# Second layer norm, denominators and Strassen-like factors of an adaLN block: some work moved between VectorE and GpSimd, some begun at other steps

## The chip, the core and the metric

The kernel runs on one core of one Trainium2 chip, in one launch. The metric is the device time of that launch in microseconds (us); smaller is better. Five engines work side by side, each with its own queue in order: TensorE (PE in the profile; its weight loads are PEld), VectorE (DVE), ScalarE (ACT), GpSimd (POOL) and SyncE (SP), which here only issues DMA transfers. An instruction at the head of a queue that waits holds up all that stands behind it on that queue.

## The reference

For a token matrix `x` of 2048 x 512 and a condition vector `c`, all in float32:

```
sa, ca, ga, sb, cb, gb = six rows of 512, from silu(c) @ w_mod
h = layernorm(x) * (1 + ca) + sa
q, k, v = h @ wqkv, in 32 heads of 16
pq, pk = phi(q), phi(k)          # phi(t) = (t + 1 if t > 0 else exp(t)) + 1e-6
kv, z = pk^T v, sum of pk        # per head, over all tokens
o = (pq kv) / (pq z + 1e-6)
x = x + ga * (o @ wo)
h = layernorm(x) * (1 + cb) + sb
x = x + gb * (((h @ w_gate) * (h @ w_up)) @ w_down)     # 1376 hidden columns
```

The attention is linear: keys and values are summed up over all tokens first, and only then are the queries used.

## The kernel before

**Precision.** Every float32 product is made of three matmuls on operands split in a high part (a rounded copy, made on ScalarE, line 181) and a low part (source minus high part, line 182, on VectorE or, where `low=` or `on=` says so, on GpSimd). A "split" below is this pair of instructions; a "low" is its second half.

**Tokens.** The 2048 tokens are 16 token tiles of 128, in 4 chunks of 4 tiles. Token tile i is tile i mod 4 of chunk i / 4.

**First stage.** First layer norm, keys and the sums over tokens. The change leaves it as it is.

**Query stage.** For each token tile: the query product (`proj`, 12 matmuls), `q_a` and `q_b` (phi, on ScalarE and VectorE), then the denominator. `den_q` (lines 511 and 485) multiplies phi with the summed keys, on GpSimd; `den_t` (lines 503 to 509) is three VectorE instructions: the sum by head (L491), the constant added (L508), the reciprocal (L509); `den_c` (L520) divides phi by the denominator, on VectorE. For chunk 0 the denominators are made earlier in another way.

**The y steps.** `y_step(i)`, line 633, is written out by hand for i = 0 to 11. In the order of the program it has: if asked for, the query product of a later tile; the turning of tile i+1 (`turn_a`, 4 transposes, L591, which need `den_c(i+1)`); `pre` and `pe` extras; `den_c(i+2)`; the output product of tile i (`y_a`, 12 matmuls, L616); high and low part of the turned tile i+1 (L595 on ScalarE, L599 on VectorE); `mid` extras; `y_b(i-1)`, which takes tile i-1 out of PSUM and makes the statistics of the second layer norm (L225, L226 on VectorE); the preload of the next accumulator (L604); and `after` extras. The lists of extras are where most of the change is made. The order of calls is the order on each queue; no scheduler changes it.

**Second layer norm.** `rstd_of` (lines 228 to 234) adds epsilon on VectorE (L233) and takes the power -0.5 on GpSimd (L234). `nmr_of` (L237) makes minus mean times rstd, on VectorE. `xhat` (L243) applies both on ScalarE. `ln2_turn` transposes 4 normalized tiles (L250), `ln2_f` (L670) scales and shifts them; chunks 2 and 3 are stored to HBM (`kept`) and read back.

**Gated products.** The two gated products are done together by a Strassen-like scheme with seven products in place of eight, in 22 blocks (`block`, line 794): two sides of 2 chunks each (side 0 is chunks 0 and 1), times 11 hidden tiles f, in groups of 2, 2, 2, 2 and 3. A side has seven left factors for two indices k: `a11`, `s1`, `s2`, `a12`, `s3`, `a22`, `s4`, where s1 to s4 are sums of quarters (`Left.sum`, L698) and each is split (`Left.split`, L181 and L182). A block has seven right factors, made of weights: `right_load`, `right_sums` (4 instructions on GpSimd, L748), `right_split` (4 high parts on ScalarE, L759 and L762; 4 lows on GpSimd, L766). In a block PE runs, 6 matmuls each (L780), the products with a11, s1, s2, a12, s3, then `pe` extras (down products of an earlier group among them, L858 to L860), then a22 and s4. Four PSUM banks hold the partial results and are copied from one to the next (L786); L832, L841 and L806 on VectorE combine them. The points `a11`, `s1`, `s2`, `s3`, `pe`, `mid`, `s4` of a block take extras from the dictionary `early` and from the loop at line 1011: `at[point]` is a list of things to issue there.

**Down products.** The rows of `w_down` are scaled at `s4` of a block (L875, VectorE) and split at `s2` of the next (`split_down`, line 966): high part on ScalarE, low part on GpSimd. `down` takes its sums out of PSUM on VectorE (L865).

**The second side.** While side 0 is being worked on, the left factors of side 1 are made in small steps (`trickle`; `some(n)` issues the next n steps) and stored in HBM (`stash`); around the change of sides (blocks 10 and 11) `fetch` reads them back. All tiles of 128x512 come from one pool of 99; a new tile waits for the last user of the one whose place it takes.

## Time and profile before

| | us |
|---|---|
| median of 3 runs (579.56 to 579.96) | 579.6 |
| the profiled execution, whole | 582.47 |
| its span, first to last instruction | 580.8 |
| PE busy in the span | 563.6 |
| VectorE busy | 376.3 |
| ScalarE busy | 294.2 |
| GpSimd busy | 236.1 |

The profile is of one execution. Its whole time is 1.67 us over its span, and 2.87 us over the median of the runs. An engine's busy time is an average over stages with different limits, so the views that matter are those by stretch of time (busy time of each engine, and the granted TensorE clock, from the span's start), the waits of PE by what ended them, the chain of work that ended last, and the order of time on single engines. Rows of groups and of the order of time give the line, engine and operation, then `out<-in` by the tiles' names, the shape and a count.

### The profile page before, as it was taken

How to read it: one execution, taken by the hardware profiler on the slowest of the kernel's cores; microseconds unless marked ns; L12 is line 12 of the kernel's file. 1: busy time of each engine (PE TensorE's matmuls, PEld its weight loads, DVE VectorE, ACT ScalarE, POOL GpSimd, SP SyncE). 2: the span in 40 equal slices, each digit the busy share in tenths (PEclk: the TensorE clock that was granted, in tenths of full speed). 3: DMA queues.
4: the chain of work that ended last, by engine and by line, in shares of the span. 5: the costliest groups of instructions: out<-in, count | busy, mean ns of one | idle time of the engine just before them, and what ended most of it. 6: DMA issues, size and time to landing. Idle time of an engine off the chain costs nothing.

```text
span 580.8 us, 7362 instructions
## 1 busy us (share of the span) xinstructions
PE 563.6 (97%) x2549; PEld 457.6 (79%) x2549; DVE 376.3 (65%) x622; ACT 294.2 (51%) x530; POOL 236.1 (41%) x237
## 2 busy tenths in 40 slices
PE   8999999999998998899999998999999999999997
PEld 6778888888777886688888886877888888888775
DVE  6886868868998688973544797564434444444643
ACT  3785766455556586553545447454323444333530
POOL 2000000005234225566564656397346666665320
PEclk9999999999998998999999999999999999999999
DMA  8900124202330011123024416599515121200003
GB/s 281 368 3 6 68 77 141 74 1 72 96 87 1 1 38 35 37 72 111 36 73 143 147 59 223 210 330 378 169 58 174 36 74 36 78 0 1 1 1 144
DMA packets 49109, 57.24 MB, mean 99 GB/s; under 512 B 6384, under 2 KB 26864, under 8 KB 49072
## 3 DMA queue, kind: packets, MB, share of 16 engines
q1 hardware_dynamic: 49072, 56.77, 30.1%
q8 instruction: 20, 0.33, 0.2%
q14 instruction: 17, 0.14, 0.1%
HBM read 43.12 MB, written 13.63 MB: 98 GB/s over the span
## 4 chain that ended last, share of the span: by engine, by line
PE 78%; DVE 12%; DMA 5%; ACT 2%; POOL 1%; issue 1%; SPq 1%; DVEq 0%; POOLq 0%
PE bank L780 31%; PE acc L859 7%; PE acc L860 7%; PE acc L858 7%; PE bank L196 5%; PE bank L194 5%; PE bank L195 5%; DVE h L182 3%; PE acc L616 2%; PE acc L327 2%; PE acc L325 2%; PE acc L326 2%; DMA h<-side_s 2%; DMA raw<-in_A_wqkv_dram 2%; PE bank L250 1%; DVE h L520 1%
## 5 line engine op out<-in xcount | busy, mean ns | idle before, releaser
L780 PE MATMUL bank<-h,w 128*128 128x512 f32 (+1 forms) x924 | 219.2, 392 | 4.5 <-DVE h L182 2.5
L780 PEld LDWEIGHTS bank<-h,w 128*128 128x128 f32 (+1 forms) x924 | 170.2, 186 | 46.8 <-DVE h L182 4.6
L786 ACT ACTIVATE bank<-bank 128x512 f32<-128x512 f32 (+1 forms) x44 | 25.6, 581 | 143.6 <-PE bank L780 143.5
L182 POOL TENSOR_TENSOR w<-raw,w 128x512 fp32r<-128x512 f32 (+1 forms) x22 | 36.8, 1675 | 116.0 <-ACT w L181 116.0
L806 DVE TENSOR_TENSOR phi<-bank,g 128x512 f32<-128x512 f32 (+1 forms) x22 | 15.2, 689 | 91.3 <-PE bank L780 91.3
L859 PE MATMUL acc<-w,kh 128*128 128x512 f32 (+1 forms) x176 | 69.3, 394 | 2.5 <-POOL w L182 2.5
L858 PE MATMUL acc<-w,kh 128*128 128x512 f32 (+1 forms) x176 | 69.3, 394 | 0.0
L860 PE MATMUL acc<-w,kl 128*128 128x512 f32 (+1 forms) x176 | 69.2, 393 | 0.0
L766 POOL TENSOR_TENSOR w<-raw,w 128x256 fp32r<-128x256 f32 (+3 forms) x44 | 45.0, 1023 | 38.2 <-ACT w L759 38.1
L766 POOL TENSOR_TENSOR w<-t,w 128x512 fp32r<-128x512 f32 (+1 forms) x44 | 57.9, 1317 | 0.0
L865 DVE TENSOR_TENSOR x<-acc,x 128x512 f32<-128x512 f32 x80 | 50.3, 681 | 9.2 <-PE acc L860 9.2
L234 POOL TENSOR_TENSOR rstd<-ve,half 128x4 f32<-128x4 f32 (+3 forms) x12 | 10.6, 883 | 106.6 <-DVE ve L233 102.4
L194 PE MATMUL bank<-w,h 128*128 128x512 f32 x120 | 48.1, 401 | 0.0
L196 PE MATMUL bank<-w,h 128*128 128x512 f32 x120 | 47.1, 392 | 0.0
L195 PE MATMUL bank<-w,h 128*128 128x512 f32 x120 | 46.7, 389 | 0.0
L485 POOL TENSOR_TENSOR f<-h,zb 128x512 f32<-128x512 f32 x12 | 17.2, 1450 | 63.7 <-ACT zb L465 50.9
L616 PE MATMUL acc<-w,xh 128*128 128x512 f32 x128 | 42.3, 412 | 0.0
L832 DVE TENSOR_TENSOR g<-bank,u 128x512 f32<-128x512 f32 (+1 forms) x22 | 15.1, 689 | 40.8 <-ACT u L786 38.9
L859 PEld LDWEIGHTS acc<-w,kh 128*128 128x128 f32 (+1 forms) x176 | 33.5, 190 | 10.0 <-POOL w L182 2.9
L858 PEld LDWEIGHTS acc<-w,kh 128*128 128x128 f32 (+1 forms) x176 | 33.5, 190 | 7.3
L860 PEld LDWEIGHTS acc<-w,kl 128*128 128x128 f32 (+1 forms) x176 | 33.3, 189 | 7.1
L243 ACT ACTIVATE n<-x,nmr,rstd 128x512 f32<-128x512 f32 x32 | 24.7, 807 | 25.9 <-DVE nmr L237 25.9
(149 smaller groups left out, 1038.7 us busy)
## 6 DMA issues: line engine op xcount, KB each, us to landing
x<-in_A_x_dram SPq DMA_DIRECT2D x24, 256.0 KB, 5.4
raw<-in_w_mod_dram SPq DMA_DIRECT2D x24, 256.0 KB, 3.6
raw<-in_B_w_gate_dram SPq DMA_DIRECT2D x40, 128.0 KB, 2.6
raw<-in_B_w_up_dram SPq DMA_DIRECT2D x40, 128.0 KB, 2.8
raw<-in_B_w_down_dram SPq DMA_DIRECT2D x20, 256.0 KB, 3.2
side_s<-h SPq DMA_DIRECT2D x16, 256.0 KB, 3.1
h<-side_s SPq DMA_DIRECT2D x16, 256.0 KB, 5.5
out_dram<-x SPq DMA_DIRECT2D x16, 256.0 KB, 2.6
```

What stands on the lines that cost most here:

```text
L182: (low or nc.vector).tensor_tensor(l, src, f32(h), op=ALU.subtract)
L194: nc.tensor.matmul(ps, ah, bh, start=i == 0, stop=False)
L195: nc.tensor.matmul(ps, ah, bl, start=False, stop=False)
L196: nc.tensor.matmul(ps, al, bh, start=False, stop=i == n - 1)
L616: nc.tensor.matmul(yps[i], x, y, start=fresh and k + n == 0, stop=k == KD - 1 and n == 2, skip_group_check=True)
L766: sub = lambda out, x, y: (on or nc.gpsimd).tensor_tensor(out, x, f32(y), op=ALU.subtract)
L780: mm = lambda x, y, **kw: nc.tensor.matmul(ps, x[:, k], y, skip_group_check=True, **kw)
L786: nc.scalar.activation(out, x, AF.Copy)
L858: nc.tensor.matmul(dn[j], hh[:n, a:b], dh[:n], start=i == 0, stop=False)
L859: nc.tensor.matmul(dn[j], hh[:n, a:b], dl[:n], start=False, stop=False)
L860: nc.tensor.matmul(dn[j], hl[:n, a:b], dh[:n], start=False, stop=i == n_of - 1)
L865: nc.vector.tensor_tensor(xt, dn[j], xt, op=ALU.add)
```

## The change

- `rstd_of` has a new argument `aside`. With it, VectorE also makes minus the mean (`nm`), and GpSimd makes `nmr` as `nm` times `rstd`, right behind the power. All calls of the second layer norm use it, and its calls of `nmr_of` and `ln2_m` go away.
- `den_c(1)` is issued before the second pair of `wo` products, where `den_c(0)` already stands. `den_t` is called for at most one token tile a step: tiles 5 and 7 come one step later than before, tile 8 two steps, tiles 9 to 12 one; the `den_q` calls are set to match.
- The sums and the split of the right factor of block 1 are issued in y steps 5 and 6; before, in y step 10 and in block 0.
- The left factors of side 0: `a11` is split in y steps 7 and 8 (before: 9); all sums s3 and s4 are on GpSimd (before: those of k = 0); s3 is summed in steps 9 and 10 and split ahead of block 0 (before: in block 0 at `s1` and `s2`); a22 is split at `s1` and `s2` (before: `s3`), s4 at `pe`, ahead of `y_a(13)`.
- The low part of the down weights is made on VectorE.
- The left factors of side 1: `a11` and `a12` are loaded in block 3 and split in blocks 3 and 4; `a21` and `a22` are loaded at `s2` of block 5; the other steps run two at a time at `s3` (from block 5 on) and at `s4` (from block 5 on). Before, everything was loaded at `s4` of block 5, and three steps ran at `s4` and, from block 6 on, at `s1`.
- The read-back around the change of sides: `a11` and `a12` in block 9, `s1`, `s2`, `s3`, `a22`, `s4` at `a11`, `s1` and `s2` of block 10.

```diff
-        def rstd_of(self, a=0, b=NJ):
+        def rstd_of(self, a=0, b=NJ, aside=False):
...
+            if aside:
+                nc.vector.tensor_scalar(self.nm[:, a:b], self.mv[:, a:b, 0], -1.0, None, op0=ALU.mult)
             nc.gpsimd.tensor_tensor(self.rstd[:, a:b], self.ve[:, a:b], half[:, a:b], op=ALU.pow)
+            if aside:
+                nc.gpsimd.tensor_tensor(self.nmr[:, a:b], self.nm[:, a:b], self.rstd[:, a:b], op=ALU.mult)
...
     q_a(9, ps)
-    den_c(0)
+    den_c(0, 1)
     w_out(2, 3)
...
-            todo = [lambda: [self.get(n) for n in ("a21", "a22", "a11", "a12")]]
-            todo += [lambda n=n: self.sum(n) for n in ("s1", "s3", "s2", "s4")]
-            return todo + [lambda n=n: self.split(n) for n in SIDE]
+            todo = [lambda n=n: self.sum(n) for n in ("s1", "s3", "s2", "s4")]
+            return todo + [lambda n=n: self.split(n) for n in ("s1", "s2", "s3", "a22", "s4")]
...
-    den_c(1)
     q_a(11, ps)
...
-    y_step(0, after=[lambda: q_b(11), lambda: den_q(7), lambda: den_t(4, 5), lambda: right_sums(0)])
-    y_step(1, after=[lambda: den_q(8), lambda: den_t(6, 7)])
-    y_step(2, after=[lambda: right_split(0), lambda: den_t(8)])
-    y_step(3, after=[lambda: n2[0].rstd_of(0, 3), lambda: den_q(9, 10)])
+    y_step(0, after=[lambda: q_b(11), lambda: den_q(7), lambda: den_t(4), lambda: right_sums(0)])
+    y_step(1, after=[lambda: den_t(5), lambda: den_q(8)])
+    y_step(2, after=[lambda: den_t(6), lambda: den_q(9), lambda: right_split(0)])
+    y_step(3, after=[lambda: den_t(7), lambda: n2[0].rstd_of(0, 3, True)])
     reload_x(8, 9, 10, 11)
-    y_step(4, q=12, pre=[lambda: n2[0].nmr_of(0, 3)], after=[lambda: n2[0].rstd_of(3, 4), lambda: n2[0].xhat(0, 1, 2), lambda: den_t(9), lambda: n2[0].nmr_of(3, 4), lambda: den_q(11)])
-    y_step(5, pre=[lambda: n2[0].xhat(3)], after=[lambda: den_t(10), lambda: den_q(12)])
-    y_step(6, pe=[lambda: ln2_turn(0, 0, 1)], after=[lambda: ln2_f(0, 0, 1), lambda: den_t(11)])
+    y_step(4, q=12, after=[lambda: n2[0].rstd_of(3, 4, True), lambda: n2[0].xhat(0, 1, 2), lambda: den_t(8), lambda: den_q(10, 11)])
+    y_step(5, pre=[lambda: n2[0].xhat(3)], after=[lambda: den_t(9), lambda: den_q(12), lambda: right_sums(1)])
+    y_step(6, pe=[lambda: ln2_turn(0, 0, 1)], after=[lambda: ln2_f(0, 0, 1), lambda: den_t(10), lambda: right_split(1)])
...
-    y_step(7, q=13, pe=[lambda: ln2_turn(0, 2, 3)], after=[lambda: n2[1].rstd_of(0, 3), lambda: ln2_f(0, 2, 3), lambda: den_t(12)])
...
-    y_step(8, pre=[lambda: n2[1].nmr_of(0, 3)], after=[lambda: n2[1].rstd_of(3, 4), lambda: den_q(13), lambda: n2[1].xhat(0, 1, 2), lambda: n2[1].nmr_of(3, 4)])
+    y_step(7, q=13, pe=[lambda: ln2_turn(0, 2, 3)], after=[lambda: n2[1].rstd_of(0, 3, True), lambda: ln2_f(0, 2, 3), lambda: den_t(11), lambda: L[0].split("a11")])
+    y_step(8, after=[lambda: n2[1].rstd_of(3, 4, True), lambda: den_q(13), lambda: n2[1].xhat(0, 1, 2), lambda: den_t(12), lambda: L[1].split("a11")])
     y_step(9, q=14, pre=[lambda: n2[1].xhat(3)], pe=[lambda: ln2_turn(1, 0, 2)], mid=[lambda: ln2_f(1, 0, 2)],
-           after=[lambda: [L[k].split("a11") for k in range(KH)], lambda: L[0].sum("s1"), lambda: den_t(13)])
+           after=[lambda: L[0].sum("s1"), lambda: den_t(13), lambda: L[0].split("a12"), lambda: L[0].sum("s3", on=nc.gpsimd)])
     y_step(10, pe=[lambda: ln2_turn(1, 1, 3)], mid=[lambda: ln2_f(1, 1, 3)],
-           after=[lambda: right_sums(1), lambda: den_q(14), lambda: L[1].sum("s1"), lambda: L[0].split("s1"), lambda: L[0].sum("s2")])
+           after=[lambda: den_q(14), lambda: L[1].sum("s3", on=nc.gpsimd), lambda: L[1].sum("s1"), lambda: L[0].split("s1"), lambda: L[0].sum("s2")])
     y_step(11, q=15, mid=[lambda: L[1].split("s1"), lambda: L[1].sum("s2")],
-           after=[lambda: L[0].split("s2"), lambda: L[0].split("a12"), lambda: den_t(14), lambda: n2[2].rstd_of(0, 3)])
-    L[0].sum("s3", "s4", on=nc.gpsimd)
+           after=[lambda: L[0].split("s2"), lambda: L[0].sum("s4", on=nc.gpsimd), lambda: den_t(14)])
     y_b(11)
     L[1].split("s2", "a12")
-    L[1].sum("s3", "s4")
+    L[1].sum("s4", on=nc.gpsimd)
+    n2[2].rstd_of(0, 3, True)
+    for k in range(KH):
+        L[k].split("s3")
...
-        split_d[s, f] = split_raw(raw_d.pop((s, f)), low=nc.gpsimd)
+        split_d[s, f] = split_raw(raw_d.pop((s, f)))
...
-        (0, "s1"): [lambda: L[0].split("s3"), lambda: turned(13), lambda: ln2_r(2, 3, 4)],
-        (0, "s2"): [lambda: L[1].split("s3")],
-        (0, "s3"): [lambda: [L[k].split("a22") for k in range(KH)]],
-        (0, "pe"): [lambda: y_a(13), lambda: [L[k].split("s4") for k in range(KH)], lambda: y_b(12)],
-        (0, "mid"): [lambda: den_q(15), lambda: den_c(14), lambda: ln2_m(2), lambda: ln2_x(2, 0)],
+        (0, "s1"): [lambda: turned(13), lambda: L[0].split("a22"), lambda: ln2_r(2, 3, 4)],
+        (0, "s2"): [lambda: L[1].split("a22")],
+        (0, "pe"): [lambda: [L[k].split("s4") for k in range(KH)], lambda: y_a(13), lambda: y_b(12)],
+        (0, "mid"): [lambda: den_q(15), lambda: den_c(14), lambda: ln2_x(2, 0)],
...
-        (3, "s2"): [lambda: ln2_m(3), lambda: ln2_x(3, 0)],
+        (3, "s2"): [lambda: ln2_x(3, 0)],
...
+        if s == 0 and n == 3:
+            second = [Left(sides[1], k).aside(stash) for k in range(KH)]
+            at["a11"].append(lambda: [l.get(x) for x in ("a11", "a12") for l in second])
+            trickle.extend(lambda x=x, l=l: l.split(x) for x in ("a11", "a12") for l in second)
         if s == 0 and n == 5:
-            second = [Left(sides[1], k).aside(stash) for k in range(KH)]
+            at["s2"].append(lambda: [l.get(x) for x in ("a21", "a22") for l in second])
             trickle.extend(x for pair in zip(*(l.steps() for l in second)) for x in pair)
-        if s == 0 and n > 5:
-            at["s1"].append(lambda: some(3))
-        if s == 0 and n >= 5:
-            at["s4"].append(lambda: some(3))
+        if s == 0 and n >= 3:
+            at["s3"].append(lambda: some(2))
+            at["s4"].append(lambda: some(2 if n > 4 else 0))
         if n:
             at["s3"].append(lambda n=n: right_split(n + 1))
-        else:
-            at["s2"].append(lambda: right_split(1))
...
+        if s == 0 and n == 9:
+            after_side = {}
+            at["pe"].append(lambda: fetch(stash, after_side, "a11", "a12"))
...
-            after_side = {}
-            fetch(stash, after_side, "a11", "s1")
-            at["a11"].append(lambda: fetch(stash, after_side, "s2", "a12"))
-            at["s2"].insert(0, lambda: fetch(stash, after_side, "s3"))
-            at["s3"].insert(0, lambda: fetch(stash, after_side, "a22", "s4"))
+            at["a11"].append(lambda: fetch(stash, after_side, "s1", "s2"))
+            at["s1"].insert(0, lambda: fetch(stash, after_side, "s3"))
+            at["s2"].insert(0, lambda: fetch(stash, after_side, "a22", "s4"))
```

More of the change, by code (lines that the diff above doesn't have):

```diff
@@ L232, in rstd_of @@
                 self.ve = T(small, "ve", (P, NJ))
+                self.nm = T(small, "nm", (P, NJ))
             nc.vector.tensor_scalar(self.ve[:, a:b], self.mv[:, a:b, 1], EPS_LN, None, op0=ALU.add)
+            if aside:
+                nc.vector.tensor_scalar(self.nm[:, a:b], self.mv[:, a:b, 0], -1.0, None, op0=ALU.mult)
             nc.gpsimd.tensor_tensor(self.rstd[:, a:b], self.ve[:, a:b], half[:, a:b], op=ALU.pow)
+            if aside:
+                nc.gpsimd.tensor_tensor(self.nmr[:, a:b], self.nm[:, a:b], self.rstd[:, a:b], op=ALU.mult)
         def nmr_of(self, a=0, b=NJ):
@@ L928, in tile_adaln_block @@
+    y_step(5, pre=[lambda: n2[0].xhat(3)], after=[lambda: den_t(9), lambda: den_q(12), lambda: right_sums(1)])
+    y_step(6, pe=[lambda: ln2_turn(0, 0, 1)], after=[lambda: ln2_f(0, 0, 1), lambda: den_t(10), lambda: right_split(1)])
+    for k in range(KH):
+        lefts[k] = Left((0, 1), k).into(side)
     right_load(2)
     reload_x(12, 13, 14, 15)
-    y_step(7, q=13, pe=[lambda: ln2_turn(0, 2, 3)], after=[lambda: n2[1].rstd_of(0, 3), lambda: ln2_f(0, 2, 3), lambda: den_t(12)])
-    for k in range(KH):
-        lefts[k] = Left((0, 1), k).into(side)
@@ L940, in tile_adaln_block @@
-    L[0].sum("s3", "s4", on=nc.gpsimd)
+           after=[lambda: L[0].split("s2"), lambda: L[0].sum("s4", on=nc.gpsimd), lambda: den_t(14)])
     y_b(11)
     L[1].split("s2", "a12")
-    L[1].sum("s3", "s4")
+    L[1].sum("s4", on=nc.gpsimd)
+    n2[2].rstd_of(0, 3, True)
+    for k in range(KH):
+        L[k].split("s3")
     trickle = []
@@ L977, in ln2_r @@
     def ln2_r(ch, a=0, b=NJ):
-        norm2[ch].rstd_of(a, b)
+        norm2[ch].rstd_of(a, b, True)
     def ln2_m(ch, a=0, b=NJ):
```

## The prediction, written before the changed kernel was built or run

> **What bounds the kernel now.** I read the page's busy times first, then busy time by stretch, then PE's waits.
>
> ```profile
> PE 563.6 (97%) x2549; PEld 457.6 (79%) x2549; DVE 376.3 (65%) x622; ACT 294.2 (51%) x530; POOL 236.1 (41%) x237
> ```
>
> PE is busy 563.6 of 580.8 us and the change leaves its matmuls alone. So it can win only PE's idle time (17.2 us) and time in which PE ran slowly. By stretch (after the length: busy time of PE, PEld, DVE, ACT, POOL, then the granted clock):
>
> ```profile
> 155.00:185.00 30.00, 27.06 (x134) 21.76 (x133) 26.90 (x51) 18.55 (x34) 11.87 (x10) 0.99 0.19 54
> 221.00:242.55 21.55, 17.28 (x65) 12.01 (x64) 19.44 (x27) 10.51 (x20) 15.66 (x13) 0.92 0.06 15
> 352.00:367.00 15.00, 12.51 (x48) 9.76 (x47) 8.46 (x15) 8.85 (x18) 9.50 (x8) 0.89 0.71 256
> ```
>
> PE idles 2.94 us in the y steps (A), 4.27 us around block 0 (B), 2.49 us in block 8 (C): 9.70 us. The other 7.5 us lie outside these stretches, which the change touches but not to PE's gain. Who ended the waits (total, times, longest):
>
> ```profile
> PE bank L591 <- DVE h L520: 2.9, 3, 1.9
> PE bank L780 <- DVE h L182: 2.5, 4, 1.3
> PE acc L859 <- POOL w L182: 2.5, 1, 2.5
> PE bank L780 <- DVE g L841: 1.5, 1, 1.5
> ```
>
> A waits for the division by the denominator, B for lows of left factors and for a bank that VectorE frees late, C for the low of a down weight on GpSimd. Each idle time is followed by a stretch at half clock:
>
> ```profile
> 181.11:184.52 3.41, 1.49 (x10) 1.01 (x9) 2.76 (x4) 1.18 (x2) 2.18 (x2) 1.00 0.00 0
> 184.52:187.94 3.42, 3.42 (x15) 3.03 (x14) 3.17 (x8) 3.42 (x8) 0.00 (x0) 0.50 0.02 5
> 225.48:228.90 3.42, 1.84 (x6) 0.67 (x4) 3.42 (x6) 2.77 (x7) 0.93 (x2) 1.00 0.00 0
> 228.90:232.31 3.41, 3.16 (x8) 2.49 (x9) 1.47 (x3) 3.13 (x7) 3.41 (x4) 0.50 0.00 0
> 358.61:362.02 3.41, 0.97 (x4) 0.84 (x5) 1.85 (x4) 3.26 (x7) 3.41 (x3) 1.00 0.81 284
> 362.02:365.43 3.41, 3.41 (x9) 2.64 (x9) 0.00 (x0) 0.11 (x1) 3.38 (x3) 0.50 1.06 405
> ```
>
> Where PE was busy for 1.84 us or less of 3.41, the next 3.41 us ran at clock 0.50, which costs half of them: 1.71 us each, 5.13 in all. The Trainium skill, "TensorE: Matmul & The Clock Gate", Part 1, says that the clock is halved after an idle window of about 3.4 us; by that, gaps of at most 2.49 us would not have halved it, these stretches would have another cause, and the sum below would be 5.13 us smaller. Here 1.58 us of idle time in a window were followed by it, so I go by the rows.
>
> **A: y steps.** The price of a step, from the chain of work (start, us, what):
>
> ```profile
> 161.90 0.60 DVE den L491
> 163.11 0.56 DVE den L491
> 164.27 0.54 DVE h L520
> 164.81 0.59 DVE xl L599
> 165.41 0.61 DVE st L225
> 166.23 0.58 DVE den L491
> 196.75 0.44 PE bank L591 x4
> 197.19 2.77 PE acc L616 x12
> ```
>
> A `den_t` costs 1.21 us (161.90 to 163.11), `den_c` and the turned low 0.6 each, the statistics 0.82. A step with one `den_t` keeps VectorE for 3.2 us, and PE for 0.44 + 2.77 = 3.2: level. Before, steps 0 to 2 carry five `den_t`, so VectorE is behind by two of them. Then GpSimd comes in:
>
> ```profile
> 176.27 1.25 DVE L237 SCALAR_TENSOR_TENSOR nmr<-mv,rstd 128x3 f32<-128x3 f32 x1 [0.96 <-POOL rstd L234]
> 180.80 1.31 DVE L508 TENSOR_TENSOR den<-den,den 128x32 f32<-128x32 f32 x1
> 182.42 0.88 DVE L237 SCALAR_TENSOR_TENSOR nmr<-mv,rstd 128x1 f32<-128x1 f32 x1
> 186.78 0.19 DVE L508 TENSOR_TENSOR den<-den,den 128x32 f32<-128x32 f32 x1
> 180.77 2.52 POOL L485 TENSOR_TENSOR f<-h,zb 128x512 f32<-128x512 f32 x2
> L234 POOL TENSOR_TENSOR rstd<-ve,half 128x1 f32<-128x1 f32 x3 | 2.0, 682 | 6.0 <-DVE ve L233 6.0
> ```
>
> L508 takes 0.19 us alone and 1.31 beside GpSimd's two L485 (1.26 each): a VectorE instruction with two inputs in SBUF stands until the GpSimd one is through.
>
> *`den_c(1)` ahead:* 0.6 us leave this queue and go to the `wo` products, where PE had no gap; if that cover is short, it costs at most the same 0.6. *One `den_t` a step:* one fewer up to step 3, 1.2 us. *`nmr` on GpSimd:* the two L237 above (2.13 us, nearly all waiting) leave VectorE; two `nm` of some 0.15 come. The GpSimd `nmr` is not in the trace: between 0.1 (all but free behind the power) and 0.7 us (L234); I take 0.5, nearest in shape. It stands behind the power it needs, so ScalarE's xhat gets it sooner than through VectorE's queue; cover gone (GpSimd late), xhat waits. That is 0.6 + 1.2 + 2.1 - 0.3 = 3.6 us against 2.94 of idle time.
>
> What is late next: `den_c(7)`. Without the first two gaps (1.02 us) PE wants the turn of tile 7 at 184.05 - 1.92 - 1.02 = 181.1. Before, that step's L508 started at 180.80; the phi ahead of it follows PE, so it starts some 1.1 sooner, at 179.7, and `den_c(7)` half a microsecond later at about 180.1, if nothing is in its way. But `den_q(10, 11)` are now both queued on GpSimd there: one wait of up to 1.26 and its own 0.6 give an end at 181.9. I leave a gap of 0.8 (ends: 0, and 1.9 as now). A wins 2.94 - 0.8 = 2.14.
>
> **B: left factors.** VectorE in block 0 before:
>
> ```profile
> 224.85 1.77 DVE L698 TENSOR_TENSOR s<-f,f 128x512 f32<-128x512 f32 x1
> 231.64 3.30 DVE L182 TENSOR_TENSOR h<-f,h 128x512 fp32r<-128x512 f32 x2
> 234.87 2.91 DVE L182 TENSOR_TENSOR h<-s,h 128x512 fp32r<-128x512 f32 x2
> 232.66 1.74 POOL L766 TENSOR_TENSOR w<-t,w 128x512 fp32r<-128x512 f32 x1
> ```
>
> Five instructions of 0.6 took 8.0 us, so 5 us went to standing behind GpSimd (sums of the left factor, then split and sums of right factors). After, the split and sums of block 1's right factor (four L766, four L748) are 40 us earlier, the s3 and s4 sums are off VectorE, and a11, a12, s3 are split before they are due. By count (0.6 an instruction, 0.8 the statistics, 1.2 a `den_t`) VectorE has about 4.0, 5.0, 3.8, 5.6 us in steps 8 to 11 and 3.4 after them, 21.8 us. PE has 20.1 in these steps (six products of 12 at 2.77, four turnings at 0.44, two layer-norm turnings at twice that) and another 9 (38 matmuls of 0.23, one turning) until s3 is wanted: 7 us to spare. GpSimd has four sums, two `den_q` and two small pairs there, some 9 us; all of it on VectorE's back would just use that up. Both banks for L841 are then freed in time, as in later blocks.
>
> What is late next: before the turn of chunk 1's tiles in step 9, ScalarE has one more split (about 0.6) ahead of the last xhat, and GpSimd the whole right split ahead of that chunk's power; I leave 0.5 (ends 0 and 2.5). B wins 4.27 - 0.5 = 3.77.
>
> The Trainium skill, "GPSIMD Engine Reference", § 4.1, would have two-input elementwise work on VectorE, GpSimd being about twice as slow, which speaks against the moved sums; by the rows a sum on GpSimd costs its 1.3 to 1.7 us off PE's path.
>
> **C: down lows and second side.** The chain into C's gap:
>
> ```profile
> 354.44 1.26 DVE h L182 x3
> 356.17 0.69 DVE raw L875
> 356.88 0.64 ACT w L181
> 357.59 3.41 POOL w L182
> ```
>
> Three low parts of the second side stand before the scaling, that before the ScalarE split, and GpSimd's low then takes 3.41 us (a free one 1.3) since VectorE's own lows keep it out. After: two steps there, scaling 0.6 earlier (355.57), then block 7's two lows, and the down low on VectorE at about 357.4 to 358.1. PE wanted it at 361.05 - 2.49 = 358.56. So C goes, with 0.5 in hand; if that fails by one GpSimd instruction, 0.8 returns. The 22 lows put 22 x 0.6 = 13 us on VectorE, which has a third of its time free, and leave GpSimd to the right factors. Behind each stands block work (L832) that waits for PE anyway. C wins 2.49.
>
> *Loads.* a21 and a22 are now wanted by sums at `s3` of block 5, while the load must follow a store made at `s2`:
>
> ```profile
> f<-kept SPq DMA_DIRECT2D x8, 256.0 KB, 4.5
> SPq L740 <- PE bank L780: 43.3, 5, 21.5
> ACT h L181 <- DMA side_a<-h: 6.7, 2, 3.4
> ```
>
> VectorE stands at these sums until the data is there, and behind it are L806 and L841, which PE wants before the third product of block 6: from the `s2` point that is 54 matmuls (a12, s3, 24 of the down product, a22, s4, a11) of 0.23, 12.4 us. Two ScalarE instructions (some 1.4), a store (I take no more than the load), a load of 4.5, two sums and two products of 0.6 make 12.8. I leave 0.5 (ends 0, for a shorter store, and 2.5, one wait of 1.3 behind GpSimd for each sum). On SP, the right factor loads queued behind these (and behind the early stores of blocks 3 and 4) come later, by up to a block; they are wanted another block after that. The earlier read-back (8 of 28 loads before block 10) takes load off SP where the old one is dense; PE lost 0.2 there, and I count nothing.
>
> **The sum.** 2.14 + 3.77 + 2.49 - 0.5 = 7.9 of idle time, and 5.1 of half clock, if no remaining gap fills its window: 13.0 us. The profiled execution took 582.5 (span 580.8); it would take 569.5. It lies 2.9 above the median of the runs, so the runs go from 579.6 to 566.6. Floor: 9.70 + 5.13 = 14.8, 564.8.
>
> **Rivals.** *GpSimd's queue becomes the wait* (0.24). From step 4 to 7 it has three `den_q`, four sums (below), four lows and then chunk 1's power, `nmr` behind it: 7 x 1.3 + 4 x 0.79 = 12.3 us in a row alone, 15.3 where the larger take the contended 1.74.
>
> ```profile
> L748 POOL TENSOR_TENSOR t<-raw,t 128x256 f32<-128x256 f32 x40 | 31.6, 789 | 1.6
> ```
>
> Then xhat comes 2.5 us late for step 9's turn, with a half-clock stretch of 1.7, and step 5 loses another 1: about 571.5. For it: L766 at 1.74 above. Against: rivals for the port on VectorE are only two a step there.
>
> *The half clock stays* (0.08), by the rule above or because what is left of the gaps still fills a window: 566.6 + 5.1 = 571.7. Against: all three stretches follow a gap.
>
> *VectorE stays behind* (0.06): the waits just move to the next low or division, and two thirds of the gain is lost: 575 to 579.
>
> *Slower: tiles run out* (0.08). Early splits and loads hold places of the 99 longer; engines then wait for PE to free a tile, in blocks 3 to 10. It decides from 13.0 / 8 = 1.6 us a block; at 2.5 the kernel takes 587. For it: SP and even ScalarE already wait for places (the last two rows above). Against: SP's waits there end long before the data is wanted.
>
> **Numbers.** The forecast, all three gaps mostly gone, has 0.54, with 564.5 to 569 as its own range. A measurement can tell about 0.2% (1.2 us) from no change. Faster: 0.54 + 0.24 + 0.08 + 0.05 = 0.91; within 0.2%: 0.01; slower: 0.08. The range 564.5 to 574 leaves out the last two rivals.
>
> **What would show it.** Right: no wait of PE for L520 over 1 us, none for left lows in block 0, none for w L182 in block 8; clock 1.00 in all three places; L508 mostly near 0.2. Wrong: PE waiting for n L243, for s L698 of GpSimd, or for L841 in block 5; ScalarE or VectorE waiting for places; half-clock stretches at new places.

## The result and the profile after

The changed kernel takes 565.6 us (median of four runs, 564.3 to 567.7) against 579.8 us for the kernel before beside it: a ratio of 0.9754, 95% interval 0.9718 to 0.979. It is faster by 2.5%. A second comparison gave 0.9752 (0.9722 to 0.9782). The forecast was 566.6 us, its range 564.5 to 574.0.

The profiled execution took 566.38 us, its span is 564.6. The span and the busy times of the changed kernel, from its page:

```profile
span 564.6 us, 7390 instructions
PE 556.7 (99%) x2549; PEld 456.0 (81%) x2549; DVE 380.2 (67%) x643; ACT 293.8 (52%) x530; POOL 207.0 (37%) x224
```

PE's idle time fell from 17.2 to 7.9 us. Busy times by stretch, columns as in the prediction, for the three places as they now lie (y steps, block 0, block 8) and for two stretches at the start:

```profile
155.00:185.00 30.00, 30.00 (x151) 24.41 (x150) 27.20 (x54) 20.97 (x40) 13.18 (x13) 1.00 0.19 54
215.00:236.00 21.00, 21.00 (x98) 17.39 (x97) 18.51 (x36) 14.30 (x26) 7.99 (x10) 1.00 0.10 26
338.00:353.00 15.00, 15.00 (x68) 12.43 (x67) 10.41 (x17) 8.26 (x16) 7.78 (x8) 1.00 0.51 181
13.27:16.68 3.41, 2.81 (x19) 2.28 (x20) 3.12 (x6) 0.63 (x1) 0.00 (x0) 1.00 1.05 386
16.68:20.09 3.41, 3.41 (x11) 2.73 (x11) 2.87 (x7) 2.82 (x5) 0.00 (x0) 0.50 1.05 386
```

In all three places PE is busy without a break and the clock is 1.00. Against that, a half-clock stretch stands at 16.68 that the profile of before did not have. All of PE's waits that are left, in the waits of the changed kernel:

```profile
PE acc L141 <- DVE w L136: 2.0, 1, 2.0
PE bank L262 <- ACT n L248: 0.9, 1, 0.9
PE acc L164 <- DVE f L159: 0.6, 1, 0.6
PE bank L784 <- DMA h<-side_s: 0.2, 1, 0.2
```

The first of these is the time before the first matmul, and the next two lie in the first 16 us. Nearly all the rest of the idle time is the 4.0 us after the last matmul. (Behind the new lines L591 is L596, L616 is L621, L780 is L784, L841 is L845, L520 is L525, L698 is L703, L859 is L863.)

**Where the time came from.** Both kernels have the same 2549 matmuls in the same order, so the k-th of one trace can be held against the k-th of the other. The difference goes from 0 to +2.0 by 18 us and settles at +1.4 (the stretch at the start), then falls to -3.4 over the y steps (A, 4.8 us), to -11.0 through block 0 (B, 7.6 us), from -11.2 to -15.8 in block 8 (C, 4.6 us), and ends at -16.1. That is 17 us from the three places and 1.4 given back at the start. The shown idle times and stretches of the prediction make 14.8 of it. Each wait costs about 0.16 us more than the view shows, because a matmul is drawn 0.39 us long while they start every 0.23; over the ten waits of the three places that is 1.6 us. The last half microsecond I cannot place, nor the other half by which the end, -16.1, lies beyond the three places.

How the critical steps now stand, from the order of time of the changed kernel, taken engine by engine (start, us, engine and line, and in brackets the idle time before and what ended it):

```profile
180.11 0.22 POOL L239 TENSOR_TENSOR nmr<-nm,rstd 128x1 f32<-128x1 f32 x1
180.29 4.25 POOL L490 TENSOR_TENSOR f<-h,zb 128x512 f32<-128x512 f32 x3
...
180.09 0.19 DVE L513 TENSOR_TENSOR den<-den,den 128x32 f32<-128x32 f32 x1
180.31 0.35 DVE L514 RECIPROCAL den<-den 128x32 f32<-128x32 f32 x1
180.58 1.55 DVE L525 SCALAR_TENSOR_TENSOR h<-h,den 128x512 f32<-128x512 f32 x1
...
182.28 0.63 PE L596 MATMUL bank<-ident,h 128*128 128x128 f32 x4
...
198.71 0.82 ACT L248 ACTIVATE n<-x,nmr,rstd 128x512 f32<-128x512 f32 x1 [0.24 <-POOL nmr L239]
...
305.99 2.48 DVE L703 TENSOR_TENSOR s<-f,f 128x512 f32<-128x512 f32 x2 [3.35 <-DMA f<-kept]
...
345.95 0.68 DVE L182 TENSOR_TENSOR w<-raw,w 128x512 fp32r<-128x512 f32 x1
```

nmr on GpSimd takes 0.22 us here, 0.20 for the first three tiles. The division of tile 7 (L525) still stands behind GpSimd's product L490, 1.55 us for 0.6, but ends at 182.13, and PE takes the turned tile at 182.28 without a wait. The fourth tile's xhat of chunk 1 ends at 199.53, 0.3 us ahead of its turn. In block 5 VectorE stands 3.35 us for the loads and PE still does not wait. The low of the down weight takes 0.68 us on VectorE.

### The profile page after: what moved, and what is told of

It is laid out like the page before. It is cut to its first block, busy times and chain, and to the rows that moved or that the text cites. A ratio compares the mean times of both kernels' runs of the same rounds, so it can differ in the third digit from the quotient of the medians.

```text
span 564.6 us, 7390 instructions
## 1 busy us (share of the span) xinstructions
PE 556.7 (99%) x2549; PEld 456.0 (81%) x2549; DVE 380.2 (67%) x643; ACT 293.8 (52%) x530; POOL 207.0 (37%) x224
## 4 chain that ended last, share of the span: by engine, by line
PE 92%; DMA 3%; DVE 3%; SPq 0%; issue 0%; ACT 0%; POOL 0%
PE bank L784 36%; PE acc L621 8%; PE acc L862 7%; PE acc L863 7%; PE acc L864 7%; PE bank L194 5%; PE bank L196 5%; PE bank L195 5%; PE acc L332 2%; PE acc L330 2%; PE acc L331 2%; PE bank L255 2%; DMA h<-side_a 1%; PE bank L596 1%; DMA x<-in_A_x_dram 1%; DMA h<-side_s 1%
## 5 line engine op out<-in xcount | busy, mean ns | idle before, releaser
L784 PE MATMUL bank<-h,w 128*128 128x512 f32 (+1 forms) x924 | 216.3, 391 | 0.2 <-DMA h<-side_s 0.2
L784 PEld LDWEIGHTS bank<-h,w 128*128 128x128 f32 (+1 forms) x924 | 170.6, 185 | 39.5 <-DMA h<-side_s 1.0
L770 POOL TENSOR_TENSOR w<-raw,w 128x256 fp32r<-128x256 f32 (+3 forms) x44 | 46.3, 1051 | 158.4 <-ACT w L763 151.1
L862 PE MATMUL acc<-w,kh 128*128 128x512 f32 (+1 forms) x176 | 68.6, 390 | 0.0
L863 PE MATMUL acc<-w,kh 128*128 128x512 f32 (+1 forms) x176 | 68.6, 390 | 0.0
L490 POOL TENSOR_TENSOR f<-h,zb 128x512 f32<-128x512 f32 x12 | 17.1, 1441 | 69.4 <-ACT zb L470 50.8
L621 PE MATMUL acc<-w,xh 128*128 128x512 f32 x128 | 40.7, 399 | 0.0
L863 PEld LDWEIGHTS acc<-w,kh 128*128 128x128 f32 (+1 forms) x176 | 33.1, 188 | 6.9
L752 POOL TENSOR_TENSOR t<-raw,t 128x256 f32<-128x256 f32 (+1 forms) x44 | 36.9, 838 | 1.7
```

Of the source, the lines that this page charges most:

```text
L621: nc.tensor.matmul(yps[i], x, y, start=fresh and k + n == 0, stop=k == KD - 1 and n == 2, skip_group_check=True)
L752: sub = lambda out, x, y: (on or nc.gpsimd).tensor_tensor(out, x, y, op=ALU.subtract)
L770: sub = lambda out, x, y: (on or nc.gpsimd).tensor_tensor(out, x, f32(y), op=ALU.subtract)
L784: mm = lambda x, y, **kw: nc.tensor.matmul(ps, x[:, k], y, skip_group_check=True, **kw)
L862: nc.tensor.matmul(dn[j], hh[:n, a:b], dh[:n], start=i == 0, stop=False)
L863: nc.tensor.matmul(dn[j], hh[:n, a:b], dl[:n], start=False, stop=False)
```

## The experiments

Each kernel is named by its label. Times are medians, with the ratio to the kernel before and its 95% interval where the kernel was timed in rounds; the kernel before had medians of 579.6 to 580.5 beside them. The diffs show only a part of each edit, and `...` stands for lines left out. First, the four parts of the change alone.

### y_only: the y steps alone

```diff
-    y_step(1, after=[lambda: den_q(8), lambda: den_t(6, 7)])
+    y_step(1, after=[lambda: den_t(5), lambda: den_q(8)])
...
-    y_step(3, after=[lambda: n2[0].rstd_of(0, 3), lambda: den_q(9, 10)])
+    y_step(3, after=[lambda: den_t(7), lambda: n2[0].rstd_of(0, 3, True)])
```

> The kernel before with only the edits to the y steps: nmr of the second layer norm on GpSimd, and the denominators' order per token tile. Theory (the three idle places are independent, and each brings its own half-clock stretch): the gaps in the y steps and the stretch after them go, the gaps in block 0 and block 8 stay; from the aligned matmuls of before and after the first place is worth 4.7 us, so about 575.1. Rival (VectorE stays behind, so that the late work only moves down into the block 0 gap): the gap in block 0 grows by what the y steps lost, and the time stays within 1 us of before, 579 to 580. The product count and the loads of this kernel are those of before.

The edit puts the denominators of tiles 5 and 6 one step later than before and those of tiles 7 and 8 two (the list of the change above has tile 7 wrong).

577.3 us, ratio 0.9933 (0.9908 to 0.9958), 3.2 us less by medians, where about 4.7 was expected. Waits of PE and, below, GpSimd's low in block 8 in the order of time:

```profile
PE bank L785 <- DVE h L182: 2.2, 3, 1.3
PE bank L785 <- DVE g L846: 1.7, 1, 1.7
PE acc L864 <- POOL w L182: 0.3, 1, 0.3
```

```profile
354.20 1.60 POOL L182 TENSOR_TENSOR w<-raw,w 128x512 fp32r<-128x512 f32 x1 [3.55 <-ACT w L181]
```

A is gone, and B (the first two lines) stays nearly as it was (3.9 us of waits), so lateness does not simply move from A into B. Against my expectation C shrank from 2.5 to 0.3 us, though nothing there was edited: GpSimd's low took 1.60 us in place of 3.40. It was set off in the same situation in both, 0.21 us after the start of a VectorE low with the same queue behind it. Here the next VectorE low stood for 1.77 us; in the kernel before it took 0.68, and GpSimd stood. One block earlier it fell the other way: from the same situation GpSimd's low took 3.43 us here, and 1.62 in the kernel before. So which of the two gets through first differs from execution to execution, and C's 2.49 us in the profile of before was one draw.

### low_only: the down lows alone

```diff
-        split_d[s, f] = split_raw(raw_d.pop((s, f)), low=nc.gpsimd)
+        split_d[s, f] = split_raw(raw_d.pop((s, f)))
```

> The kernel before with one edit: the low parts of the down product's factor are made on VectorE and not on GpSimd. Theory (the lateness in block 8 comes from the three second-side lows that stand before the scaling on VectorE, and GpSimd's 3.41 us is only its last part): the low part now queues on VectorE behind three further second-side lows of about 1 us each and ends near 360.4 in place of 361.0; PE's gap in block 8 shrinks from 2.5 to about 1.9 us, the half-clock stretch stays, and the time is within 1 us of before (578.7 to 579.8). Rival (the starved GpSimd instruction is the whole cause): the gap and its stretch go, 4.6 us less, 575.2.

581.1 us, ratio 1.0014 (0.9993 to 1.0035): no gain. The chain of work in block 8:

```profile
353.54 1.80 DVE h L182 x3
355.35 0.60 DVE raw L875
355.95 1.20 DVE kl L182 x2
357.15 1.81 DVE h L182 x3
358.96 0.61 DVE w L182
```

The low itself now takes 0.6 us, but stands behind three more second-side lows (357.15) in VectorE's queue. PE's gap was 1.52 us, where 1.9 was expected, and one of 0.33 came in block 6. The half-clock stretch that was expected to stay did not come: the grid cut the gap into 0.49 and 1.03 us. The starved GpSimd instruction was not the whole cause.

### side_only: the second side alone, down lows still on GpSimd

```diff
-        if s == 0 and n > 5:
-            at["s1"].append(lambda: some(3))
-        if s == 0 and n >= 5:
-            at["s4"].append(lambda: some(3))
+        if s == 0 and n >= 3:
+            at["s3"].append(lambda: some(2))
+            at["s4"].append(lambda: some(2 if n > 4 else 0))
```

> The kernel before with only the second side's edits: two of its loads and splits from block 3 on, its steps spread as two at s3 and two at s4, the loads of a21 and a22 in block 5 and the read-back in block 9; the down lows stay on GpSimd. Theory (three second-side lows ahead of the scaling in block 8 make the factor late): the gap in block 8 falls below 0.8 us and has no half-clock stretch, 4 to 4.6 us less, 575.2 to 575.8. Rival (the low part on GpSimd is the cause, whatever stands ahead of it): a gap of about 2 us stays with its stretch, 579 to 580.

578.1 us, ratio 0.9956 (0.9934 to 0.9979). PE has no wait in block 8. GpSimd's low there took:

```profile
356.90 1.61 POOL L182 TENSOR_TENSOR w<-raw,w 128x512 fp32r<-128x512 f32 x1 [4.34 <-ACT w L181]
```

So the spread steps close C without the move of the lows. One short draw would not show that alone, but a long one had no occasion here: VectorE had nothing to do from 357.36 to 358.31, and none of the 22 down lows took over 1.61 us, where the kernel before and `y_only` each have two of 3.40 us or more. The gain by medians, 2.5 us, is less than the 4.2 that C and its stretch cost in the profile of before, as it must be if C was a high draw there. This trace also shows the wait of 1.92 us of the y steps, unchanged, fall across two windows; the last two rows are of block 0:

```profile
180.97:184.39 3.42, 2.55 (x12) 1.75 (x10) 3.35 (x6) 1.51 (x3) 2.75 (x3) 1.00 0.00 0
184.39:187.80 3.41, 2.25 (x15) 1.95 (x16) 2.61 (x6) 3.08 (x6) 0.28 (x1) 1.00 0.00 0
...
225.35:228.76 3.41, 1.87 (x7) 0.85 (x5) 3.41 (x6) 2.77 (x7) 0.92 (x2) 1.00 0.00 0
228.76:232.17 3.41, 3.18 (x8) 2.33 (x8) 1.47 (x3) 3.13 (x7) 3.41 (x4) 0.50 0.00 0
```

No half-clock stretch followed the cut wait. In `left_only` the grid cut the same wait into about 0.9 and 1.1, in `low_only` into 1.84 and 0.09, and none followed there either. In block 0, several short waits that add up to 1.54 us in one window did bring one.

### left_only: the left factors and right factor 1 alone

```diff
-           after=[lambda: right_sums(1), lambda: den_q(14), lambda: L[1].sum("s1"), lambda: L[0].split("s1"), lambda: L[0].sum("s2")])
+           after=[lambda: den_q(14), lambda: L[1].sum("s3", on=nc.gpsimd), lambda: L[1].sum("s1"), lambda: L[0].split("s1"), lambda: L[0].sum("s2")])
...
-        (0, "s1"): [lambda: L[0].split("s3"), lambda: turned(13), lambda: ln2_r(2, 3, 4)],
+        (0, "s1"): [lambda: turned(13), lambda: L[0].split("a22"), lambda: ln2_r(2, 3, 4)],
```

> The kernel before with only the earlier left factors (a11, a12, s3 split sooner, s3 and s4 sums on GpSimd) and the earlier sums and split of right factor 1; nmr stays on VectorE and the denominators in their old order. Theory: the waits of block 0 and their half-clock stretch go, the y steps' gaps and block 8's stay; the place is worth 7.6 us by the aligned matmuls, so about 572.2. Rival (the left factors are late only because VectorE comes out of the y steps late): a gap of 2 us or more and a stretch stay in block 0, 576 to 579.

573.2 us, ratio 0.9872 (0.9833 to 0.9912), 7.4 us less. Waits of PE, and the low in block 8:

```profile
PE bank L591 <- DVE h L520: 2.9, 3, 1.9
PE acc L859 <- POOL w L182: 0.7, 1, 0.7
```

```profile
350.38 1.60 POOL L182 TENSOR_TENSOR w<-raw,w 128x512 fp32r<-128x512 f32 x1 [4.24 <-ACT w L181]
```

B is gone with A in place: VectorE's lateness in the y steps does not make B. C shrank again, GpSimd's low having drawn 1.60 us. By medians the four parts give 3.2, -0.6, 2.5 and 7.4 us, 12.5 together; the whole change gave 14.2. Within the intervals that adds up. Next, single parts undone. The changed kernel was timed in other rounds than these, so differences to it of less than about 2 us rest on the waits in the traces, not on the medians.

### nmr_back: nmr on VectorE again

```diff
-    y_step(3, after=[lambda: den_t(7), lambda: n2[0].rstd_of(0, 3, True)])
+    y_step(3, after=[lambda: den_t(7), lambda: n2[0].rstd_of(0, 3)])
...
-    y_step(4, q=12, after=[lambda: n2[0].rstd_of(3, 4, True), lambda: n2[0].xhat(0, 1, 2), lambda: den_t(8), lambda: den_q(10, 11)])
+    y_step(4, q=12, pre=[lambda: n2[0].nmr_of(0, 3)], after=[lambda: n2[0].rstd_of(3, 4), lambda: n2[0].xhat(0, 1, 2), lambda: den_t(8), lambda: n2[0].nmr_of(3, 4), lambda: den_q(10, 11)])
```

> The changed kernel with one part undone: nmr of the second layer norm is made by one VectorE instruction again, at its old places. Theory (nmr on VectorE stands behind the power and the products on GpSimd, and tile 7's division is the next thing in that queue): VectorE loses about the 2.1 us that L237 took before, against some 0.15 us of slack that the division of tile 7 has in the changed kernel; a gap of 1 to 2 us returns ahead of the turn of tile 7, with or without a half-clock stretch, 567 to 569.5. Rival (the denominators' new order is what closed the gap, nmr hides): no gap over 0.3 us, within 0.7 us of the changed kernel's 565.6.

568.0 us, ratio 0.9812 (0.978 to 0.9844), 2.4 us more than the changed kernel. One wait of PE for L525 is back, 1.03 us ahead of the turn of tile 7. VectorE and GpSimd there, in the order of time:

```profile
179.45 1.31 DVE L513 TENSOR_TENSOR den<-den,den 128x32 f32<-128x32 f32 x1
181.06 0.91 DVE L242 SCALAR_TENSOR_TENSOR nmr<-mv,rstd 128x1 f32<-128x1 f32 x1
181.90 0.68 DVE L525 SCALAR_TENSOR_TENSOR h<-h,den 128x512 f32<-128x512 f32 x1
...
179.42 4.31 POOL L490 TENSOR_TENSOR f<-h,zb 128x512 f32<-128x512 f32 x3
```

L513 takes 1.31 us and nmr 0.91, where L513 took 0.19 in the changed kernel and the division alone stood behind GpSimd. The denominators' order, which this kernel keeps, accounts for the rest of A (2.94 down to 1.03), and nmr for the last microsecond.

### right1_back: right factor 1 late again

```diff
-    y_step(5, pre=[lambda: n2[0].xhat(3)], after=[lambda: den_t(9), lambda: den_q(12), lambda: right_sums(1)])
+    y_step(5, pre=[lambda: n2[0].xhat(3)], after=[lambda: den_t(9), lambda: den_q(12)])
...
+        else:
+            at["s2"].append(lambda: right_split(1))
```

> The changed kernel with one part undone: the sums of block 1's right factor in y step 10 and its split in block 0 again. Theory (the left lows in block 0 were late because VectorE stood behind GpSimd's four lows and four sums there): left lows at 1.2 to 1.8 us in place of 0.68, PE waits 1 to 3 us in block 0 for lows or for L845, 567 to 571. Rival (the earlier splits of the left factors are enough, and the right factor is only carried along): no wait over 0.3 us in block 0, within 0.7 us of 565.6.

568.1 us, ratio 0.9808 (0.9781 to 0.9836), 2.5 us more than the changed kernel. Waits of PE and the place in the order of time:

```profile
PE bank L784 <- DVE g L845: 0.8, 1, 0.8
PE bank L784 <- DVE h L182: 0.7, 1, 0.7
```

```profile
225.70 3.52 DVE L182 TENSOR_TENSOR h<-s,h 128x512 fp32r<-128x512 f32 x2
...
226.92 1.75 POOL L770 TENSOR_TENSOR w<-t,w 128x512 fp32r<-128x512 f32 x1
```

Two left lows take 3.52 us beside the right factor's lows, and PE waits 1.5 us: by this, the late right factor was about a third of B.

### sums_dve: the s3 and s4 sums on VectorE

```diff
-           after=[lambda: L[0].sum("s1"), lambda: den_t(13), lambda: L[0].split("a12"), lambda: L[0].sum("s3", on=nc.gpsimd)])
+           after=[lambda: L[0].sum("s1"), lambda: den_t(13), lambda: L[0].split("a12"), lambda: L[0].sum("s3")])
```

(and the same for the other three).

> The changed kernel with all four s3 and s4 sums of side 0 on VectorE. Theory (VectorE has about 7 us to spare by my count for steps 8 to 11 and block 0, and four sums cost it 2.4): no gap over 0.3 us, 565.6 within 0.7. Rival (VectorE's own load was the cause, and the sums are what had to leave it): gaps of 1 to 2.4 us in block 0, 567 to 570.

565.7 us, ratio 0.9767 (0.9736 to 0.9799), as the changed kernel. Behind the start PE has no wait at all. That these sums went to GpSimd bought nothing.

The remaining runs look at the clock and at the margins.

### late_bank: waits of set sizes

```diff
+        for _ in range(late):
+            nc.vector.tensor_tensor(extra[:n], c, c22[:n], op=ALU.mult)
```

> The changed kernel with extra work that no output needs: in blocks 11 to 20, VectorE makes 4, 5, 6, 7, 5, 6, 4, 7, 5 and 6 products of 0.6 us more ahead of L845, which frees the bank that PE's next product takes. So PE gets a gap of 1.0, 1.6, 2.2 or 2.8 us a block (some 19 us in all). Theory (the clock is halved for one window of 3.41 us whenever PE idled about half of the window before it, on a fixed grid): gaps of 1.0 never bring a stretch, gaps of 1.6 and 2.2 do only where most of them falls in one window, gaps of 2.8 nearly always; the limit lies between 1.2 and 1.9 us of idle time in a window. Rival (what counts is one unbroken pause of 1.6 us or more, wherever it falls): every gap of 2.2 and 2.8 is followed by a stretch and no window of several short waits is. Second rival (a whole idle window of 3.4 us is needed): none of these gaps brings one.

602.3 us. Ten gaps came, of 1.52 to 3.70 us, where 1.0 to 2.8 were expected. Windows on the grid (busy time of PE first, the granted clock third from the end):

```profile
435.28:438.69 3.41, 1.26 (x6) 1.09 (x7) 3.34 (x6) 1.01 (x2) 0.00 (x0) 1.00 0.02 5
438.69:442.10 3.41, 3.41 (x10) 2.64 (x9) 3.41 (x6) 0.28 (x1) 0.00 (x0) 0.50 0.00 0
...
527.44:530.85 3.41, 1.54 (x7) 0.94 (x5) 3.24 (x6) 1.12 (x2) 0.44 (x1) 1.00 0.00 0
530.85:534.26 3.41, 1.58 (x7) 1.34 (x8) 3.34 (x6) 0.63 (x1) 0.00 (x0) 1.00 0.00 0
534.26:537.68 3.42, 3.42 (x17) 2.82 (x16) 3.42 (x7) 1.96 (x4) 0.00 (x0) 1.00 0.00 0
```

A pause of 3.70 us that the grid cut into 1.87 and 1.83 brought no stretch. A pause of 2.25 us that lay in one window (547.92) did. Five of the ten gaps brought one, each with 2.0 to 2.3 us of idle time in one window; 1.58 did not. The rival of one unbroken pause falls by the 3.70 gap, the rival of a whole idle window by all five. The Trainium skill, "TensorE: Matmul & The Clock Gate", Part 1, has the window at 3413 ns and free-running, and every stretch here agrees (3.41 us, at another phase in each execution); its "no PE-idle gaps >~3.4µs" does not agree with a stretch after 2.0 us.

### pool_more: GpSimd's queue lengthened in step 5

```diff
+            nc.gpsimd.tensor_tensor(scratch, zb, zb, op=ALU.mult)
...
-    y_step(5, pre=[lambda: n2[0].xhat(3)], after=[lambda: den_t(9), lambda: den_q(12), lambda: right_sums(1)])
+    y_step(5, pre=[lambda: n2[0].xhat(3)], after=[lambda: den_t(9), lambda: den_q(12), lambda: pool_more(3), lambda: right_sums(1)])
```

> The changed kernel with three more products of 128x512 on GpSimd in y step 5, ahead of the sums of block 1's right factor (work that no output needs; 3.9 us alone, up to 5.2 beside VectorE). Theory (GpSimd's queue ahead of chunk 1's power has some 2.8 us to spare in the changed kernel: 1.0 us of idle time ahead of the power, and xhat done some 1.8 us before PE turns it): xhat comes 1 to 2.5 us late for the turn in step 9, and the gap is that, with a half-clock stretch only where it falls in one window; 566.5 to 569.5. Rival (the queue is nowhere near the path): no wait over 0.3 us, 565.6 within 1.

567.9 us. Waits of PE, and GpSimd and ScalarE in the order of time:

```profile
PE acc L621 <- ACT acc L609: 0.7, 1, 0.7
PE bank L255 <- ACT n L248: 0.5, 1, 0.5
```

```profile
184.05 3.60 POOL L927 TENSOR_TENSOR phi<-zb 128x512 f32<-128x512 f32 x3
...
191.03 0.63 ACT L766 ACTIVATE w<-t 128x512 fp32r<-128x512 f32 x1 [0.68 <-POOL t L752]
193.69 0.58 ACT L609 ACTIVATE acc<-x 128x512 f32<-128x512 f32 x1
```

Both waits are short and no stretch followed. The longer one is not the xhat that I had watched: ScalarE's high parts of the right factor (L766) wait for the late sums, and behind them on ScalarE stands the preload of the accumulator (L609) for PE's next product. The xhat is 0.5 us late, not 1 to 2.5.

### load_late: block 5's loads 2 us later

```diff
-            at["s2"].append(lambda: [l.get(x) for x in ("a21", "a22") for l in second])
...
+            at["s3"] += [lambda n=n: right_load(n + 3), lambda: [l.get(x) for x in ("a21", "a22") for l in second]]
```

> The changed kernel with block 5's loads of a21 and a22 issued at s3 behind the loads of a right factor, some 2 us later. Theory (VectorE stands 3.4 us at the sums for these loads already, and L845 behind them has about 0.6 us to spare): PE waits 1 to 1.8 us for L845 in block 5 or 6, 566.5 to 569. Rival (the loads have room, since another engine holds the bank): no wait over 0.3 us there, 565.6 within 1.

568.1 us. The sums in block 5 in the order of time, and two windows:

```profile
307.07 2.13 DVE L703 TENSOR_TENSOR s<-f,f 128x512 f32<-128x512 f32 x2 [5.91 <-DMA f<-kept]
```

```profile
308.32:311.74 3.42, 1.60 (x7) 1.04 (x6) 3.39 (x6) 1.79 (x3) 0.33 (x1) 1.00 0.03 11
311.74:315.15 3.41, 3.41 (x9) 2.63 (x9) 3.41 (x6) 0.18 (x2) 0.00 (x0) 0.50 0.29 77
```

A gap of 1.82 us and a stretch, 3.7 us by the aligned matmuls. This execution had no stretch at the start, which hides part of that in the whole time. The view of waits names ScalarE's L181 as what ended the gap, but that ended only 0.06 us after L845 of VectorE, and it is L845 that frees the bank of PE's next product. L845 began at 309.73, 0.74 us later than in the changed kernel, while PE was 1.64 us earlier there: 2.4 us later by PE's count made 1.82 of wait, so this place has about half a microsecond to spare.

### start_full, beside the changed kernel again

```diff
-    keep_on(18)
+    keep_on(20)
...
-    keep_on(1)
+    keep_on(4)
```

> The changed kernel as it is, timed beside the next ones. Theory (its runs differ only by how the fixed grid of the clock falls on the start, where a half-clock stretch of one window, of two windows or none follows the waits at 8 and 15 us, 0 to 2 us): a median of 565.6 within 0.8 and single runs from 564 to 568. Rival (the runs differ by the y steps or the blocks): a profile with a gap over 0.5 us behind 20 us.

> The changed kernel with five more filler matmuls of 0.23 us at the start (2 and 3, whose results nobody reads), where PE waits 0.9 us at 8.4 and 0.6 us at 15.3. Theory (the half-clock stretch at 14 to 20 us follows a window in which PE idled 0.6 us and ran matmuls of one column for some 1.8 us, and these hardly count as work): with the idle time filled the stretch comes seldom or never, the median falls by 0.5 to 1.5 us and the runs lie closer together, 564.1 to 565.1. Rival (the matmuls of one column alone bring it, or the start is bound by VectorE and the clock there is hidden): within 0.4 us of the changed kernel, same spread.

The changed kernel: 565.6 us (565.0 to 567.5), ratio 0.9752 (0.9722 to 0.9782), no gap behind 20 us over 0.22 us, and in its profile a half-clock stretch of two windows at the start. `start_full`: 565.2 us (564.7 to 566.2), ratio 0.9749 (0.9722 to 0.9777). Windows at the start of `start_full`:

```profile
13.46:16.87 3.41, 3.07 (x24) 2.55 (x22) 3.01 (x6) 0.63 (x1) 0.00 (x0) 1.00 1.04 381
16.87:20.28 3.41, 3.41 (x10) 2.73 (x10) 3.02 (x8) 3.03 (x5) 0.00 (x0) 0.50 1.04 378
```

With 0.34 us of idle time in the window the stretch still comes. The lower median is within what the runs differ by, so no better version is shown. What is left in that window are matmuls of one column (L164), drawn 0.25 us long and started every 0.11; that they count for little is the reading that fits, but no run took them away.

## Why the prediction was right

The verdict, the places and the mechanism of A and B held. The sum came near the time partly because errors of both signs met.

- **What bounds the kernel.** Right: PE's waits of three places went, and the time with them. The 7.5 us outside the three places stayed (7.9 now).
- **A.** Both parts were needed: without nmr's move 1.03 us remain (`nmr_back`). nmr on GpSimd was taken as 0.5 us and measures 0.20 to 0.22. The gap of 0.8 that I left for the division of tile 7 did not come. The division did stand behind a `den_q`, the first of the two (1.55 us), but VectorE started it sooner than I had it, and it ended 0.15 us ahead of its turn.
- **B.** Right in mechanism, and `right1_back` shows the standing behind GpSimd that I counted from the rows (3.52 us for two lows). The count of 7 us to spare on VectorE is borne out by `sums_dve`: it takes four sums more and PE does not wait. So taking the s3 and s4 sums off VectorE, which stands among the reasons for B's gain, was worth nothing. The Trainium skill, "GPSIMD Engine Reference", § 4.1, whose rule spoke against these sums on GpSimd, is not decided by it: 565.7 against 565.6 us, since both engines have the time. The 0.5 left for the late xhat did not come; its margin is 0.3 us. The rest of B beyond right factor 1 falls to the earlier splits by difference; they were not run alone.
- **C.** The step that failed in part is "GpSimd's low then takes 3.41 us ... since VectorE's own lows keep it out", read as a fixed cost. It is a draw: 1.60 us in two other kernels with the same queue, and in one of these 3.43 a block earlier, where the kernel before drew 1.62. And the move of the low to VectorE, which the step has as part of the cure, is worth nothing alone (`low_only`, 1.52 us of gap left), while the spread steps are enough alone (`side_only`). The Trainium skill, "GPSIMD Engine Reference", § 1, says that GpSimd shares its SBUF interfaces with VectorE instructions that have two SBUF inputs; the rows agree, and add that either side may be the one that stands.
- **Loads.** I had the data 0.4 us late and left 0.5; no wait came, and `load_late` puts the margin at about half a microsecond. The term was off by some 0.9 us, within its ends. (The bank that L841 frees is taken by the second product of block 6, not the third; the count of 54 matmuls has it right.)
- **Half clock, 5.1 us.** Right for the profiled execution, where all three stretches went, and wrong as a price for the median: the same wait of 1.92 us brought a stretch in the kernel before and none in three others, where the grid cut it. That the profile of before lay 2.9 us over its median fits with its three stretches and its long draw of C; I carried the whole 13.0 over to the median. The granted clock of single runs bears this out: among eleven runs of the kernel before it is 0.999 at the fastest, 577.95 us, and 0.991 at the slowest, 583.16.
- **The sum.** From profile to profile I had 13.0 us, 582.5 to 569.5; it was 16.1, to 566.4: 1.8 from the gaps that I left and that did not come, 2.7 from what the waits cost beyond their shown idle time (1.6) and from what I cannot place, less 1.4 for the stretch at the start, which I had not looked for. Against these 3.1 us more, the profile of before stood 2.9 over its median and that of after 0.8. The difference, 1.0 us, is how far the forecast lay above the time.
- **The rivals.** GpSimd's queue did not become the wait, but the rival was close: 3.6 us more of it cost two waits (`pool_more`), the longer by a way that I had not named. Half clock did not stay, VectorE was not left behind, and tiles did not run out: PE's longest wait in the 22 blocks is 0.2 us.

## What to carry to other kernels

Look at what stands behind an instruction on its queue before moving it to another engine: the down low is two to five times as fast on VectorE by its rows (0.68 us against 1.60 or 3.40) and the move alone gained nothing, while spreading out the three lows ahead of it closed the gap without the move. Take an instruction's long duration beside GpSimd as one of two outcomes, and a half-clock stretch as a chance that a wait of about 2 us runs, before carrying either from one profile to a median. Where a place is closed, find its margin (here 0.15, 0.3 and 0.5 us), since the next change will spend it.

## What the runs showed of the hardware

- **The clock goes by windows on a fixed grid, not by the length of a pause.** The grid is 3.41 us, with another phase in each execution. A single wait that lay within one window brought a half-clock stretch from 1.82 us of shown idle time on, and none up to 1.58. Pieces of 1.83, 1.84 and 1.87 us of a wait that the grid cut brought none, but in block 0 several short waits brought one with only 1.54 to 1.61 us in a window (`side_only`, the kernel before, `low_only` and `y_only`), so shown idle time has no clean limit. PE's work has one, by an estimate from the rows that counts a matmul of 512 columns as the 0.23 us after which the next one starts, and a transpose as 0.11. Between 20 us and the last matmul, in all fourteen traces, each of the twelve full-clock windows with up to 1.33 us of such work was followed by half clock, and none with 1.38 us or more was.
- **Windows with little idle time can still be followed by half clock** where they hold matmuls of one column: 0.34 us of idle time at the start of `start_full` was enough. Executions had none, one or two half-clock windows at the start, worth 0 to 2.5 us by the aligned matmuls, which would be most of the spread between runs of the changed kernel.
- **VectorE and GpSimd, both with two SBUF inputs, can hold up each other in either direction.** Set off 0.21 us behind a VectorE low, GpSimd's 128x512 low took 3.40 us once and 1.60 twice; in the latter cases a VectorE low took 1.77 in place of 0.68. In the long case it ended 1.13 us after the last of the three VectorE lows queued there, so it stood until all of them were through. What decides it the runs do not show.
